# Attention weights of two batches turned by DMA in two float16 parts, batch 0 masked like the others, and the second w_out read once

## The chip, the cores and the metric

One core of one Trainium2 chip. The metric is the device time of one execution in microseconds (us); the time given for a kernel is the median of several runs.

## What is computed

Attention over 4 batches of 8 heads, 576 positions, 64 columns per head: heads 0 to 3 look at the last 32 positions (local), heads 4 to 7 at every 32nd (strided). Its output, 2304 tokens of 512 columns, goes through two layers of two products each, 512 to 2048 and back.

```python
scores = np.where(masks, scale * (q @ k.T), -1e9)      # per head
attn = np.exp(scores - scores.max(-1)); attn /= attn.sum(-1) + 1e-9
x = attn @ v                                           # (2304, 512)
h = x @ w_in;  x = np.maximum(0.01 * h, h) @ w_out     # first layer (moe)
h = x @ w_in2; x = (np.maximum(h, 0) + np.log1p(np.exp(-abs(h)))) @ w_out2
```

The weights arrive as 64-bit floats.

## The kernel before

The accuracy asked for is that of float32, so each large product is made of three float16 products, of a high and a low part of each side (`mm3`, lines 543 to 546). The weights are cut into such parts on the core: a quarter of a matrix (2 MB) is loaded, its largest value found (L169), its words shifted and merged (L175, L214 to L235), and the high and low parts written (L243, L250 to L258).

The attention of a batch goes in six halves: three local ones of four tiles of 96 rows by 128 columns for each of two partition groups, and three strided ones with tiles of 126, 108 and 108 rows (`spec`, L329). A half goes through these steps, each on its engine:

- `dots` (TensorE, L346): scores in float32, into a PSUM pair.
- `top` (VectorE, L381): the row maxima. In mode "e" a masked minimum (L395) also writes the masked, negated scores to a buffer `s` in SBUF, of which there are two. Batch 0 has the modes "pppaaa" instead: the mask is added on TensorE by a matmul (L362), VectorE takes one reduction for the whole half (L387), and in "p" TensorE lowers the scores by the maxima in PSUM (`lower`, L412).
- `expo` or `expos` (ScalarE, L437, L419): exponentials, per tile with the row sums in "e" and "a", in one instruction for the half in "p", where VectorE sums afterwards (L435).
- `guard`, `norm` (VectorE), `spread` (GpSimd, L466): division by the sums, L469.
- `turn` (TensorE, L471): float32 transposes of the weights into PSUM (L478), `fetch` (ScalarE, L481): a copy to SBUF (L489).
- `pv` (TensorE, L492): the output, L501; `high` and `rest` (L526, L533) cut it into float16 parts, the input of the first layer.

The first layer takes the 8 units of 288 tokens in turn: `plan_first` (L905) projects up (tile h), `plan_second` and `plan_second_by_f` project down (tile o). The second layer takes 9 units of 256 tokens (class `Unit`, L1190), with seven products in place of eight in its second matmul, for which sums of the quarters of w_out are cut into parts as well (L1095 to L1160). Its w_out is read twice: `plan_largest` (L877) loads all four quarters for one largest value, and the loop at L1147 loads each once more.

The order of the work is written out at build time: the class `Plan` (L585) simulates the engines with the costs that stand beside each step, and at each moment takes the ready step of the lowest rank (RANKS, L40: a start and a slope per kind of step). Each engine and SP's DMA queue then carries out its list in that order, and each step waits for what it reads. Where the plan finds TensorE idle in the first 130 us it puts in filler matmuls (`idle`, L97); ten more run at the start (WARM). The plan counts 2.6 us from the end of a load's queue time to its landing (LOAD, L588).

Of the kernel before, what the change touches and what calls it, by code (L numbers as in the profile page):

```python
# [9 lines left out]
BF16 = mybir.dt.bfloat16  # L10
# [22 lines left out]
SETS = [(0, 2), (2, 2), (4, 1)]  # L33
NEG = -8.0e9
TINY = 2.0 ** -100
WARM = 10
# [22 lines left out]
MODES = ("pppaaa","eeeeee","eeeeee","eeeeee")  # L59
# [4 lines left out]
def build(tc, qt, kl, ks, v, wi1, wo1, wi2, wo2, mloc, mstr, out):  # L64
    nc = tc.nc
    with ExitStack() as ctx:
# [37 lines left out]
        ml = const.tile([BLK, 4, WIN], BF16, name="ml")  # L104
        ms = const.tile([P, 234], BF16, name="ms")
        nc.scalar.dma_start(ml, mloc)
        nc.scalar.dma_start(ms, mstr)
# [160 lines left out]
        class Attn:  # L268
            def __init__(self, b):

                self.b, self.mode = b, MODES[b]
                self.q, self.k = {}, {}
                self.ps, self.sm, self.st, self.sv = {}, {}, {}, {}

            def load_qk(self, p, q=None, k=None):
                b = self.b
                w = S + STR if p < 2 else S
# [3 lines left out]
                nc.sync.dma_start(q[:, :S], qt[b, p])  # L281
# [47 lines left out]
            def spec(self, half):  # L329

# [1135 lines left out]
```

## Time and profile before

| | |
|---|---|
| median of 3 runs | 839.45 us (839.22 to 839.84) |
| the profiled execution | 838.91 us |
| its span, first to last instruction | 837.1 us |
| granted TensorE clock, mean | 0.998 of 2.4 GHz |
| TensorE matmuls busy | 825.3 us, 99% |
| VectorE busy | 486.1 us, 58% |
| ScalarE busy | 523.3 us, 63% |
| GpSimd busy | 256.0 us, 31% |

The profile names lines of the kernel before, engines and tiles. PE is TensorE, DVE VectorE, ACT ScalarE, POOL GpSimd, SP the queue that issues the loads and stores. The end of a matmul is modelled, so that neighbours overlap; the time that a group of matmuls takes on the engine is read from its start to the start of the next.

### The profile page before, as it was taken

The numbers are of one execution on the slowest core, as the hardware profiler recorded it, in microseconds if no ns is written. First come the engines' busy times: TensorE is split into PE (matmuls) and PEld (weight loads), VectorE is DVE, ScalarE is ACT, GpSimd is POOL, SyncE is SP. The second block draws the span as 40 slices with busy tenths as digits, with TensorE's granted clock in tenths as the row PEclk, the third lists the DMA queues.
The fourth block names the chain that finished last, engine by engine and source line by source line (L and its number), as shares of the span: only waits on it lengthen the run. The fifth ranks groups of instructions, "written<-read, shape, count | busy, mean of one in ns | idle before, by whom it ended". The sixth has DMA issues, their size and how long they took to land.

```text
span 837.1 us, 17534 instructions
## 1 busy us (share of the span) xinstructions
PE 825.3 (99%) x7323; PEld 681.8 (81%) x7323; DVE 486.1 (58%) x1134; ACT 523.3 (63%) x961; POOL 256.0 (31%) x193
## 2 busy tenths in 40 slices
PE   9999999999999999999999999999999999999997
PEld 4567777787788787777777888888888888888886
DVE  5999759630433262577535567867474755565453
ACT  2898958233765465135535398877667677787671
POOL 2248786112334432002414033222322232222220
PEclk9999999999999999999999999999999999999999
DMA  9934130300225520450202200000000000000000
GB/s 369 381 130 160 60 143 1 139 1 1 65 92 220 202 101 16 187 188 16 101 2 101 101 2 1 27 1 27 1 27 1 27 1 27 26 2 26 2 26 26
DMA packets 10991, 63.27 MB, mean 76 GB/s; under 512 B 1344, under 2 KB 1440, under 8 KB 7840
## 3 DMA queue, kind: packets, MB, share of 16 engines
q1 hardware_dynamic: 10656, 62.00, 19.6%
q8 instruction: 57, 0.93, 0.5%
q14 instruction: 22, 0.18, 0.1%
q10 hardware_dynamic: 256, 0.16, 0.1%
HBM read 57.44 MB, written 4.72 MB: 74 GB/s over the span
## 4 chain that ended last, share of the span: by engine, by line
PE 85%; ACT 5%; DMA 5%; DVE 4%; issue 0%; SPq 0%; POOL 0%; DVEq 0%; ACTq 0%
PE o L544 13%; PE o L546 13%; PE o L545 13%; PE h L544 13%; PE h L546 13%; PE h L545 13%; DMA v<-v_dram 3%; PE po L501 2%; PE ps L367 2%; PE pt L478 1%; DMA pair<-wi_dram 1%; ACT s L447 1%; ACT gr L1281 1%; DVE pair L224 1%; DVE pair L1317 1%; DVE pair L235 1%
## 5 line engine op out<-in xcount | busy, mean ns | idle before, releaser
L544 PE MATMUL h<-x,w 128*128 128x256 f16 (+1 forms) x1088 | 303.5, 279 | 0.9 <-ACT t L565 0.9
L546 PE MATMUL h<-x,w 128*128 128x256 f16 (+1 forms) x1088 | 303.4, 279 | 0.0
L545 PE MATMUL h<-x,w 128*128 128x256 f16 (+1 forms) x1088 | 303.4, 279 | 0.0
L1269 POOL TENSOR_TENSOR pair<-pair,t 128x512 f32<-128x512 f32 x72 | 93.9, 1304 | 270.7 <-ACT t L1265 123.2
L571 POOL TENSOR_TENSOR g<-t,g 128x576 f16<-128x576 f32 x64 | 99.9, 1567 | 202.4 <-ACT g L568 202.4
L546 PE MATMUL o<-g,pair 128*128 128x288 f16 x512 | 146.4, 286 | 0.8 <-DVE pair L258 0.8
L544 PE MATMUL o<-g,pair 128*128 128x288 f16 x512 | 146.5, 286 | 0.0
L545 PE MATMUL o<-g,pair 128*128 128x288 f16 x512 | 146.4, 286 | 0.0
L1285 DVE SCALAR_TENSOR_TENSOR gr<-pair,x2b,gr 128x896 f16<-128x896 f32 x72 | 87.2, 1212 | 83.5 <-ACT gr L1281 83.3
L545 PEld LDWEIGHTS <-w 128*128 128x128 f16 x1088 | 106.5, 98 | 19.7 <-issue 1.0
L544 PEld LDWEIGHTS <-w 128*128 128x128 f16 x1088 | 106.4, 98 | 19.6
L546 PEld LDWEIGHTS <-w 128*128 128x128 f16 x1088 | 106.4, 98 | 19.2
L1277 DVE TENSOR_TENSOR pair<-pair 128x128 f32<-128x128 f32 x288 | 71.7, 290 | 36.1 <-POOL pair L1269 33.6
L1281 ACT ACTIVATE gr<-pair,x2b 128x896 f16<-128x896 f32 x72 | 74.4, 1035 | 17.8 <-DVE pair L1277 15.2
L565 ACT ACTIVATE t<-h,gs 128x576 f32<-128x576 f32 x64 | 47.2, 737 | 60.6 <-PE h L546 55.5
L1252 ACT ACTIVATE t<-h,x2s 128x512 f32<-128x512 f32 x72 | 49.0, 680 | 52.0 <-PE h L546 52.0
L469 POOL TENSOR_TENSOR s<-s,sm 96x512 f32<-96x512 f32 (+3 forms) x48 | 47.8, 1016 | 89.9 <-DVE sm L464 40.6
L545 PE MATMUL o<-w,gr 128*128 128x256 f16 x270 | 73.6, 273 | 0.0
L544 PE MATMUL o<-w,gr 128*128 128x256 f16 x270 | 73.6, 273 | 0.0
L546 PE MATMUL o<-w,gr 128*128 128x256 f16 x270 | 73.6, 273 | 0.0
L169 DVE TENSOR_REDUCE m<-pair 128x1 f32<-128x2048 f32 x16 | 36.4, 2276 | 52.7 <-DMA pair<-wo_dram 37.6
L546 PEld LDWEIGHTS <-pair 128*128 128x128 f16 x512 | 50.1, 98 | 13.8 <-DVE pair L258 1.1
(134 smaller groups left out, 1367.7 us busy)
## 6 DMA issues: line engine op xcount, KB each, us to landing
pair<-wo_dram SPq DMA_DIRECT2D x12, 2048.0 KB, 8.1
pair<-wi_dram SPq DMA_DIRECT2D x8, 2048.0 KB, 10.9
out_dram<-pair SPq DMA_DIRECT2D x18, 256.0 KB, 2.1
q<-qt_dram SPq DMA_DIRECT2D x12, 288.0 KB, 4.0
v<-v_dram SPq DMA_DIRECT2D x2, 1408.0 KB, 14.9
pair<-v_dram SPq DMA_DIRECT2D x2, 1408.0 KB, 7.1
k<-ks_dram SPq DMA_DIRECT2D x7, 288.0 KB, 4.9
k<-kl_dram SPq DMA_DIRECT2D x5, 304.0 KB, 3.9
```

Of the source, the lines that this page charges most:

```text
L169: nc.vector.tensor_reduce(out=m, in_=hi.bitcast(F32), axis=AX.XY, op=ALU.max, apply_absolute_value=True)
L469: nc.gpsimd.tensor_tensor(out=sv, in0=sv, in1=rs, op=ALU.mult)
L544: nc.tensor.matmul(ps, ah, bh, start=first, stop=False)
L545: nc.tensor.matmul(ps, ah, bl, start=False, stop=False)
L546: nc.tensor.matmul(ps, al, bh, start=False, stop=last)
L565: nc.scalar.activation(t, ps, AF.Prelu, scale=gates[f // 4], alpha=0.01)
L571: nc.gpsimd.tensor_tensor(out=g[:, 1, f : f + 2, :], in0=t, in1=g[:, 0, f : f + 2, :], op=ALU.subtract)
L1252: nc.scalar.activation(t, self.ps[k], AF.Prelu, scale=self.sc[:, k // 2 : k // 2 + 1], alpha=-1.0)
L1269: nc.gpsimd.tensor_tensor(out=r, in0=r, in1=self.a[k], op=ALU.add)
L1277: nc.vector.tensor_tensor(out=r[:, o], in0=r[:, x], in1=r[:, y], op=op)
L1281: nc.scalar.activation(self.a[k][:, 0], self.r[k][:, 1:], AF.Copy, scale=self.ag)
L1285: nc.vector.scalar_tensor_tensor(out=a[:, 1], in0=self.r[k][:, 1:], scalar=self.ag, in1=a[:, 0], op0=ALU.mult, op1=ALU.subtract)
```

## The change

Six things.

1. Batches 2 and 3 (TURNED) have no `turn` and `fetch`. After `spread`, `cut` writes the weights of a half as float16 (ScalarE), `remain` the rest as a second float16 part over the bytes of the buffer `s` (VectorE), and `cross` turns each part by a transposing DMA on SP's queue, from SBUF to a region behind the batch's v. `join` adds the two turned parts back to float32 (VectorE), and `pv` reads that. One such region exists (place "tr"). The buffer `s` is held until `pv`; before it was held until the second `turn`. Strided tiles are read with 128 columns and 128 or 112 rows, and `guard`, `factor`, `high` and `rest` carry the scale in another place.
2. Batch 0 has mode "e" in all halves, so that the masks and the lowering on TensorE go.
3. The first loads of q and k are split: the columns of the first two local tiles first (`load_early`, k on ScalarE's queue), the rest later (`load_late`). WARM is 8, and the plan lets TensorE begin at 4.4 in place of 5.7.
4. `plan_largest` goes: each quarter of the second w_out is loaded once, with its own largest value, scale and broadcast matmul; the ratio of the scales is put on the activations (`self.ag` per quarter).
5. Some buffers move (q and k of batches 0 and 1, parts of the second w_out).
6. All ranks are new, and with them the order of the work.

Code for smaller tiles (SMALL, an empty tuple) is added and not used; it is left out below.

```diff
-WARM = 10
+WARM = 8
+TURNED = (2, 3)
+PAD = 20
 RANKS = {
-    "A2": (1411.761, 0.020), "B2": (870.957, 132.683), "B3": (-3104.685, 0.471), ...
+    "A2": (921.068, 0.024), "B2": (1213.392, 0.020), "B3": (-892.057, 7.138), ...
-MODES = ("pppaaa","eeeeee","eeeeee","eeeeee")
+MODES = ("eeeeee",)*4
...
+            def load_early(self):
+                for p, masks in ((0, [(mn, msml)]), (1, [(ml, mloc), (ms, mstr)])):
+                    self.q[p], self.k[p] = (get() for get in self.spots[p])
+                    n, m = 2 * BLK, 2 * BLK + STR
+                    nc.sync.dma_start(self.q[p][:, :n], qt[0, p][:, :n])
+                    nc.scalar.dma_start(self.k[p][:, :m], kl[0, p][:, :m])
+                    for mask in masks:
+                        nc.scalar.dma_start(*mask)
...
                 t0, nt = SETS[half - 3]
-                r = CLS[t0] * NJ
-                return r, r, [
+                r = w = CLS[t0] * NJ
+                if self.turned:
+                    r, w = -(-r // 16) * 16, P
+                return r, w, [
...
+            def cut(self, half):
+                r, w, tiles = self.spec(half)
+                n = len(tiles)
+                hi = att.tile([P, 512], F32, name="a", tag="aT", bufs=3)
+                self.hl[half] = both = [y.bitcast(F16)[:, : 2 * n * P] for y in (hi, flat(self.s[half]))]
+                self.cuts = [y[:r].rearrange("p (j n w) -> p j n w", j=2, n=n)[:, :, :, :w] for y in both]
+                nc.scalar.activation(self.cuts[0], self.sv[half], AF.Copy)
+
+            def remain(self, half):
+                hi, lo = self.cuts
+                nc.vector.tensor_tensor(out=lo, in0=self.sv[half], in1=hi, op=ALU.subtract)
+
+            def cross(self, half, i):
+                r, w, tiles = self.spec(half)
+                n, rows = len(tiles), -(-r // 16) * 16
+                y = self.hl[half][i]
+                t = self.hl[half][i] = self.across[:, i, : 2 * n * rows].rearrange("p (n r) -> p n r", r=rows)
+                nc.sync.dma_start_transpose(t, y[:rows])
+
+            def join(self, half):
+                r, w, tiles = self.spec(half)
+                n, (hi, lo) = len(tiles), self.hl[half]
+                a = flat(self.s[half])[:w, : 2 * n * r].rearrange("p (n r) -> p n r", r=r)
+                nc.vector.tensor_tensor(out=a, in0=hi[:w, :, :r], in1=lo[:w, :, :r], op=ALU.add)
+                for j in range(2):
+                    self.st[2 * half + j] = a[:, n * j : n * j + n]
...
-                clock = collections.defaultdict(float, SP=1.4, PE=5.7)
+                clock = collections.defaultdict(float, SP=1.4, PE=4.4)
...
+                if A.turned:
+                    y = [step("Pool", 0.05 + n / 4, A.spread, [norm], half, j) for j in range(2)]
+                    y = step("ACT", 0.12 + c / 1200, A.cut, y, half, take=["a"])
+                    y0 = step("SP", 0.8, A.cross, [y, ld["v"]], half, 0, take=["tr"], behind=chain["tr"])
+                    chain["tr"] = [y0]
+                    y1 = step("DVE", 0.1 + c / 960, A.remain, [y], half, port=True)
+                    y1 = step("SP", 0.8, A.cross, [y1], half, 1, behind=[y0])
+                    y1 = step("DVE", 0.1 + 2 * n * r / 960, A.join, [y0, y1], half, port=True, free=[y, y0])
+                    pv = step("PE", 0.1 + 0.19 * n, A.pv, [y1, ld["v"]], half, take=["po"], free=[held])
...
-        def plan_largest(W, name, busy):
...
-        o2_scaled = plan_largest(O2, "O2", busy)
...
+            ld = plan.add("SP", 5.15, lambda q=q: O2.load(q, area(1)), busy[1], ("LO2", q))
+            x = plan.add("DVE", 2.2, big, [ld], ("O2", q))
+            y = plan.add("PE", 0.06, over, [x], ("O2", q), take=["pt"])
+            sc = plan.add("DVE", 1.1, scale, [y], ("O2", q + 0.3), free=[y])
+            o2_scaled.append(sc)
             y = step("DVE", 1.14, lambda q=q: O2.low(q), [ld], 0.1)
-            y = sink(step, O2, q, lambda: late["o2s"], [y, o2_scaled], 0.3)
+            y = sink(step, O2, q, lambda st=st: st["s"], [sc, x, y], 0.3)
```

## Rows read from the trace of the kernel before

**Rows 1.** The page: engine, busy us, share of the span, instructions.

```profile
PE 825.3 (99%) x7323; PEld 681.8 (81%) x7323; DVE 486.1 (58%) x1134; ACT 523.3 (63%) x961; POOL 256.0 (31%) x193
```

**Rows 2.** Stages: window, length, busy us (instructions) per engine, clock, DMA share, GB/s.

```profile
0.00:61.00 61.00, 56.98 (x469) 33.72 (x470) 50.07 (x134) 39.84 (x124) 18.30 (x23) 1.00 0.76 300
61.00:92.00 31.00, 30.09 (x295) 23.99 (x296) 29.40 (x81) 27.05 (x77) 23.20 (x16) 1.00 0.30 111
...
180.00:255.00 75.00, 74.83 (x723) 60.26 (x721) 22.97 (x163) 45.18 (x162) 22.35 (x22) 1.00 0.19 64
...
300.00:335.00 35.00, 35.00 (x358) 27.89 (x356) 18.69 (x83) 20.78 (x63) 7.56 (x8) 1.00 0.05 12
335.00:540.00 205.00, 204.84 (x1739) 169.61 (x1737) 125.29 (x189) 112.26 (x137) 45.07 (x30) 1.00 0.19 74
```

**Rows 3.** Waits of TensorE, the longest: us in total, times, longest.

```profile
PE pt L478 <- ACT a L489: 1.7, 5, 0.6
```

**Rows 4.** Timeline of TensorE, first and last turn behind the front: start, length.

```profile
181.21 0.50 PE L478 MATMUL pt<-ident,s 96*128 96x96 f32 x4
181.63 1.12 PE L367 MATMUL ps<-k,q 64*96 64x128 f32 x16
...
330.19 0.35 PE L478 MATMUL pt<-ident,s 108*108 108x108 f32 x2
330.38 0.29 PE L544 MATMUL o<-g,pair 128*128 128x288 f16 x1
```

**Rows 5.** The first 61 us, three lines alone: filler L101, masks L362, lowering L412.

```profile
0.00:61.00 61.00, 22.82 (x84) 8.00 (x84) 1.00 0.76 300
...
0.00:61.00 61.00, 3.35 (x12) 1.29 (x12) 1.00 0.76 300
...
0.00:61.00 61.00, 5.57 (x12) 1.79 (x12) 1.00 0.76 300
```

**Rows 6.** Timeline of the front: first issue, filler, scores, reduction, first projection.

```profile
0.74 0.37 SPq L281 DMA_DIRECT2D v<-qt_dram  x1
...
1.62 5.14 PE L101 MATMUL idle<-idb 128*128 128x512 bf16 x15 [1.62 <-DVE idb L92]
...
7.13 1.12 PE L367 MATMUL ps<-v 64*96 64x128 f32 x16
...
8.29 1.22 DVE L387 TENSOR_REDUCE mx<-ps 96x8 f32<-96x1024 f32 x1 [6.73 <-PE ps L367]
...
54.84 0.30 PE L544 MATMUL h<-x,w 128*128 128x288 f16 x1
```

**Rows 7.** Groups by form: line, engine, shapes, count, busy us, mean ns.

```profile
L435 DVE TENSOR_REDUCE sm<-s 96x8 f32<-96x1024 f32 x3 | 3.6, 1209 | 0.0
L387 DVE TENSOR_REDUCE mx<-ps 96x8 f32<-96x1024 f32 x3 | 3.6, 1203 | 7.1 <-PE ps L367 7.1
...
L447 ACT ACTIVATE s<-s,mx 96x128 f32<-96x128 f32 x72 | 27.8, 389 | 0.0
...
L425 ACT ACTIVATE s<-ps 96x1024 f32<-96x1024 f32 x3 | 3.1, 1019 | 11.8 <-PE ps L412 11.8
L447 ACT ACTIVATE s<-ps,mx 126x126 f32<-126x126 f32 x8 | 2.8, 374 | 0.0
```

**Rows 8.** Timeline of VectorE: two masked minima in a row.

```profile
40.24 0.28 DVE L395 CUSTOM_DVE_ANT_0 s<-ps,ml 96x128 f32<-96x128 f32 x1
40.45 0.28 DVE L395 CUSTOM_DVE_ANT_0 s<-ps,ml 96x128 f32<-96x128 f32 x1
```

**Rows 9.** Landing of 288 KB loads (L281, 200 to 260 us), then of 256 KB stores (L1336).

```profile
DMA to landing us min/median/max: 2.8/3.3/5.0
...
DMA to landing us min/median/max: 2.0/2.1/3.1
```

**Rows 10.** The page's DMA issues: KB each, us from issue to landing.

```profile
v<-ks_dram SPq DMA_DIRECT2D x1, 288.0 KB, 7.8
```

**Rows 11.** Groups of GpSimd: the division by the sums.

```profile
L469 POOL TENSOR_TENSOR s<-s,sm 96x512 f32<-96x512 f32 (+3 forms) x48 | 47.8, 1016 | 89.9 <-DVE sm L464 40.6 <-DVE g L137 29.3 <-ACT s L447 11.7
```

More of the change, by code (lines that the diff above doesn't have):

```diff
@@ L366, in dots @@
                         js = slice(D * j, D * j + D)
+                        if self.small:
+                            for o in range(2):
+                                nc.tensor.matmul(
+                                    pv[js, o, i, :], self.q[p + o][js, q0 : q0 + QT], self.k[p + o][js, k0 : k0 + w],
+                                    start=not masked, stop=not masked or i == n - 1,
+                                )
+                            continue
                         nc.tensor.matmul(
@@ L475, in turn @@
                 pt = ps_pt.tile([P, 512], F32, name="pt", tag="pt")
+                self.st[2 * half + j] = pt
+                if self.small and half > 2:
+                    for i in range(n):
+                        o = i * w - (QT - w) * (i == n - 1)
+                        for h in range(2):
+                            hs = slice(QT * h, QT * h + QT)
+                            nc.tensor.matmul(
+                                pt[hs, QT * i : QT * i + QT], sv[hs].rearrange("p n w -> p (n w)")[:, o : o + QT], ident[hs, hs],
+                                start=True, stop=True,
+                            )
+                    return
                 ptv = pt[:w, : n * r].rearrange("p (n r) -> p n r", n=n)
@@ L717, in plan_loads @@
                 if n == "v":
-                    ld[n] = plan.add("SP", 3.4, lambda: A.load_v(buf()), after.get("v", ()), (f"L{b}", k))
+                    ld[n] = plan.add("SP", 4.6 if A.small else 3.4, lambda: A.load_v(buf()), after.get("v", ()), (f"L{b}", k))
+                    continue
+                if b == 0 and n < 2:
+                    A.spots = where
+                    cost, load = ((0.43, A.load_early), (2.3, A.load_late))[n]
+                    ld[n] = plan.add("SP", cost, load, after.get(n, ()), (f"L{b}", k), behind=[ld[0]] if n else [])
                     continue
@@ L875, in plan_quarter @@
             return step("DVE", 2.3, lambda: W.rest(q), [y], 0.6, port=True), sc
-        def plan_largest(W, name, busy):
-            m = once(lambda: sml.tile([P, 4], F32, name="m4", tag="wm4"))
-            st, read = {}, []
-            for q in range(4):
-                ld = plan.add("SP", 5.15, lambda q=q: W.load(q, area(1)), busy[1], ("L" + name, q))
-                y = plan.add("DVE", 2.2, lambda q=q: W.largest(q, m()[:, q : q + 1]), [ld], (name + "l", q))
-                busy[1] = [y]
-                read.append(y)
-            def over():
-                st["m"] = sml.tile([P, 1], F32, name="m", tag="wm")
-                nc.vector.tensor_reduce(out=st["m"], in_=m(), axis=AX.X, op=ALU.max)
-            def all_over():
-                st["g"] = to_all(st["m"])
-            def scale():
-                late["o2s"] = keep([P, 1], "s_o2")
-                nc.vector.tensor_copy(late["o2s"], W.scale_all(largest_of(st["g"])))
-            step = lambda eng, cost, fn, deps, **kw: plan.add(eng, cost, fn, deps, (name + "l", 4), **kw)
-            t = step("DVE", 0.1, over, read)
-            t = step("PE", 0.1, all_over, [t], take=["pt"])
-            return step("DVE", 1.1, scale, [t], free=[t])
         gs, xs = {}, {}
@@ L1181, in w2_join @@
         def w2_join():
+            c, m = late["co"], late["uo"] = keep([P, 4], "c_o2"), keep([P, 1], "u_o2")
+            for q in range(4):
+                nc.vector.tensor_copy(c[:, q : q + 1], O2.u[q])
+            r = sml.tile([P, 1], F32, name="r", tag="jr")
+            nc.vector.tensor_reduce(out=m, in_=c, axis=AX.X, op=ALU.max)
+            nc.vector.reciprocal(out=r, in_=m)
+            nc.vector.tensor_scalar(out=c, in0=c, scalar1=r, scalar2=None, op0=ALU.mult)
             late["u2"] = keep([P, 4], "u_w2")
```

296 lines of the change are left out of this document (206 added, 90 removed), and 20 rows, old and new, of the table RANKS.

## The prediction

> **What bounds the kernel now.** I read the page's busy shares first, then the busy time stage by stage, then the waits, then single stretches of the timeline. TensorE is busy for 825.3 of 837.1 us [rows 1]. That share alone does not show that its work is useful, so the stages come next [rows 2]: from 92 us to the end TensorE is full (74.83 of 75, 35.00 of 35, 204.84 of 205 in the three stretches shown), while VectorE and ScalarE have room in the stretches that hold the attention of batches 2 and 3 (VectorE 22.97 of 75 and 18.69 of 35 us). The waits agree: the largest that TensorE spends on another engine is 1.7 us in total, for the copy of turned weights [rows 3]. So behind the front every instruction taken from TensorE is worth its own slot, and every wait put in front of one costs its length.
>
> The front is different. Up to 61 us TensorE is "busy" with 84 filler matmuls (22.82 us), 12 mask matmuls (3.35) and 12 lowering matmuls (5.57) [rows 5]; the first projection starts at 54.84 [rows 6]. There VectorE is the full engine (50.07 of 61 us, idle until 8.29; then 29.40 of 31), with ScalarE close behind from 61 us on (27.05 of 31) [rows 2, 6]. TensorE work removed from the front is replaced by filler and gains nothing by itself; the front shortens only if the first projections come earlier.
>
> **The base.** The profiled execution took 838.91 us, 1.81 beside its span of 837.1; the median of the runs is 839.45, 0.54 above it. I change the trace by differences and take them off the median.
>
> **Part 1, turning by DMA in batches 2 and 3.** Removed from TensorE: 24 groups of transposes at L478. The first starts at 181.21 and the next instruction at 181.63, so it takes 0.42 us; the last takes 330.38 - 330.19 = 0.19 [rows 4]. Over all 24 groups these slots, from one start to the next, add up to 9.0 us; the busy times beside them (0.50 and 0.35) are longer because their modelled ends overlap the next instruction. All of it lies where TensorE is full: -9.0. Removed with them are 24 copies at L489, off the path.
>
> Added to TensorE: strided scores grow from 126 and 108 to 128 columns and strided outputs from 126 and 108 to 128 and 112. A group of 16 score matmuls at 128 columns takes at most 1.12 us [rows 4]. One set of a batch is short by 2 of 128 columns and two by 20 of 128, and the last is half as large: about 0.25 us per batch, 0.5 for both (0.3 to 0.8).
>
> Added elsewhere, twelve times: a cast of 1,024 columns on ScalarE (the nearest row, L425 of that size, 1.02 us), a subtraction and an addition on VectorE (a 1,024-column operation, L435, 1.21 us) [rows 7], and two transposing DMAs on SP's queue. The ScalarE casts (12) roughly repay the removed copies. VectorE gets 12 x 2.2 = 26 us in stretches where it stood idle for 68 of 110 us [rows 2]. Hidden.
>
> What is not hidden for certain is **latency**. The output matmuls of a half now wait for scores, VectorE, ScalarE, GpSimd (two at 1.02 us [rows 11]), cast, two DMAs and an addition, and they stand in an order written out by the planner. Whatever is behind them on TensorE, projections that are ready included, waits with them. The planner prices a transpose at 0.8 us of queue and 2.6 to land, 3.4 in all. No transposing DMA is in this trace. The nearest rows: 288 KB loads in this same stretch land 2.8 to 5.0 us after issue, median 3.3, and 256 KB stores 2.0 to 3.1, median 2.1 [rows 9]; the slowest of that size, stuck behind others at the start, took 7.8 [rows 10]. A transpose moves 192 KB within SBUF in a local half, 256, 224 and 112 in the three strided ones. Two score buffers keep two halves in flight, so lateness L - 3.4 shows at every second output group: 12 x (L - 3.4) / 2 = 6 x (L - 3.4). At 2.0 or 3.3 us this is 0, at 5.0 it is 9.6, at 7.8 it is 26.4. I take L = 3.7, since the loads of this stretch are the nearest row and a transpose is likely to be a little worse than a copy: +2 (0 to 26).
>
> SP's queue also holds these waits: the second transpose of a half waits for VectorE, and the loads of batch 3 and of the second layer's weights stand behind it. They have tens of us until use, so 0.
>
> **Part 2, batch 0 like the others, first loads split.** Masks and lowering leave TensorE in the front: 0 by themselves. On VectorE a local half cost two reductions, 1.20 + 1.21, and now costs eight masked minima at 0.21 (40.24 to 40.45) = 1.68: 0.7 less in each of three halves [rows 7, 8]. The strided halves I take as even (0.7 either way). ScalarE pays: a local half cost one exponential of 1.02 and now costs eight of 0.389, so 3 x 2.09 = 6.3 more, and the strided 20 some 0.3 more: +6.6 [rows 7]. It fits into the part of the front where ScalarE waits (39.84 of 61 us busy), unless it lands after 40 us. The start: filler runs from 1.62 for 5.14 us, the first scores start at 7.13 and VectorE's first reduction at 8.29 [rows 6]. Two fillers fewer and no mask matmul, with 96 KB pieces to wait for in place of four 288 to 304 KB loads, put this some 1.5 to 2.5 us earlier. The two k pieces and three masks, one of them unused, are now five issues of about 0.4 us on ScalarE's queue; its first exponential is later than 8.29, so they hide. VectorE is continuously loaded after it, so its gain is 2 + 2.2 = 4; I take -3.5 for the start of the projections, with -8 and +4 as ends. The better end is a front in which VectorE does batch 0 and the first quarter of the weights before anything of batch 1; the worse has ScalarE's 6.6 us on the path, less the start.
>
> **Part 3, w_out of the second layer read once.** Four loads of 2 MB go; the four reductions stay but move into each quarter, with three more scale steps and three more broadcast matmuls. These matmuls are smaller than a pair of turns, 0.19 [rows 4]: at most 0.6, taken as 0.3. TensorE loses 0.16 us in 335 to 540 [rows 2], so fewer loads can give no more than that; taken as 0. The cover is the first layer's last units. If it failed, TensorE would wait at the new broadcast matmul of a late quarter for VectorE, a few reductions of 2 us long.
>
> **Sum.** 839.45 - 9.0 + 0.5 + 0.3 - 3.5 = 827.75; with +2 of stalls, **829.8 us**.
>
> By a rule of the Trainium skill, "VectorE: DVE Perf Modes", section "The three transpose paths", one 128 x 128 bf16 transpose takes 390 ns on TensorE and 1,309 ns by DMA, and its "Rules for kernel authors" prefer TensorE where PSUM will do. The page's time for eight such blocks in a row would be an estimated 10.5 us, and the sum with it 827.75 + 6 x 7.1 = 870. No run here shows a transposing DMA yet.
>
> **Rivals.**
>
> *The transposes are late (slower).* If the queue handles the 128-column blocks of a transpose as DMAs of their own, eight issues of 0.37 us each [rows 6] take 3.0 before the last can land in 2.1 to 3.3: L = 5.1 to 6.3. The loss is 6 x 1.7 = 10 to 6 x 2.9 = 17, up to 26 at the slowest row: 838 to 854, 845 in the middle. It decides from L = 3.4 + 11.7 / 6 = 5.35 us. For it speaks that every output group has TensorE's whole queue behind it; against it that plain transfers of this size land in 2 to 5 us. Chance 0.25, of which 0.01 faster, 0.05 the same, 0.19 slower.
>
> *Blocks wholly one after the other (slower).* Each of eight waits for the one before to land, at least 8 x 2.0 = 16 us if like the shortest store: 6 x 12.6 = 76, some 900 us; at half that, about 855. The skill's section above bears on this one. Chance 0.04.
>
> *ScalarE takes over the front.* It is already full from 61 to 92 us [rows 2]. If the added 6.6 us fall there and only the early start of 2 is kept, the front is 4 longer: 827.75 + 3.5 + 4 = 835, with stalls 837. Still faster. Chance 0.12. This also stands for new ranks that order the front worse than the old ones.
>
> *A better front.* The end of -8 and no stalls: 823, down to 819. Chance 0.08.
>
> **How the numbers follow.** The forecast (824 to 835) has 0.51. About 0.2%, 1.7 us, is what a measurement of this kernel can tell from no change. Faster: 0.51 + 0.01 + 0.12 + 0.08 = 0.72; same 0.05; slower 0.19 + 0.04 = 0.23. The range goes from 819 to 848: it leaves out the upper part of the late transposes, the serial ones and a little of the better front, some 0.15.
>
> **What would show it.** Right: no transposes on TensorE behind the front; output matmuls of batches 2 and 3 with waits of some tenths of a us; transposing DMAs landing in 3 to 4 us; the first projection near 51 us; VectorE's first masked minimum near 6. Wrong in the large term: TensorE waits of a us or more for the addition after the second transpose, at up to twelve places, or filler-free idle slots between 180 and 335 us. Wrong in the front: a first projection later than 55 us, or TensorE gaps until 92 us that end with ScalarE. Wrong in part 3: TensorE waiting for a reduction of w_out between 335 and 540 us.

## The result, and the profile after

| | before | after |
|---|---|---|
| median | 839.59 us | 849.04 us (847.35 to 851.22) |
| ratio, 95% interval | | 1.0115 (1.0095 to 1.0136) |
| profiled execution, its span | 838.91, 837.1 us | 847.35, 845.3 us |
| TensorE matmuls busy | 825.3 us | 818.2 us |

(The 839.59 of before are from runs on the same chip.) The kernel is 1.15% slower. TensorE has 7.1 us less to do and takes 8.2 us longer. The page's line of busy times after the change, and the windows of [rows 2] again (window, length, busy us of PE, PEld, which is the weight load, DVE, ACT and POOL, then clock, DMA share, GB/s):

```profile
PE 818.2 (97%) x7228; PEld 672.8 (80%) x7228; DVE 519.6 (61%) x1280; ACT 531.1 (63%) x994; POOL 271.9 (32%) x193
```

```profile
0.00:61.00 61.00, 52.60 (x411) 32.03 (x412) 43.63 (x173) 41.25 (x138) 20.04 (x22) 0.94 0.80 313
61.00:92.00 31.00, 29.29 (x266) 22.25 (x265) 29.39 (x80) 28.01 (x65) 25.96 (x11) 1.00 0.34 121
180.00:255.00 75.00, 73.72 (x689) 57.59 (x688) 35.02 (x148) 38.34 (x121) 22.13 (x19) 1.00 0.27 62
300.00:335.00 35.00, 34.40 (x295) 27.02 (x291) 18.59 (x37) 20.05 (x34) 14.01 (x12) 1.00 0.43 140
335.00:540.00 205.00, 198.39 (x1674) 163.06 (x1673) 134.92 (x226) 106.25 (x130) 42.06 (x29) 1.00 0.14 52
```

Two windows stand out against [rows 2]: the first, where VectorE gets 6.4 us less done (43.63 for 50.07) and the clock is 0.94, and the last, where TensorE had 0.16 us of gaps and now has 6.6. The waits of TensorE over the whole run (us in total, times, longest), in place of the 1.7 of [rows 3]:

```profile
PE ps L409 <- DVE mx L447: 5.3, 3, 3.9
PE pm L142 <- DVE m L179: 4.8, 2, 3.1
PE po L611 <- DVE s L585: 2.9, 4, 1.0
```

L409 are the scores, L447 the masked minimum, L142 a broadcast matmul, L179 the largest value of a quarter, L611 the output, L585 the addition of the turned parts.

Where the time goes is read best from a count. Both kernels start the same projection matmuls (6,312 recorded in each, L544 to L546 before, L676 to L678 after). The start of the n-th after the change less that before is the lag at that point. At n = 600 the same share of the attention is done in both (192 of 352 score matmuls, 176 of 352 output matmuls), at n = 2000 all of it.

| n-th projection matmul | 0 | 200 | 600 | 1000 | 2000 | 2800 | 3000 | last |
|---|---|---|---|---|---|---|---|---|
| before, us | 54.8 | 92.9 | 142.0 | 193.5 | 345.3 | 443.4 | 467.9 | 831.1 |
| lag after | -3.6 | -5.6 | +5.1 | +3.9 | +1.0 | +3.7 | +8.7 | +8.2 |
| lag, mask first | -9.3 | -11.7 | -1.0 | -2.3 | -4.7 | -1.6 | +5.5 | +5.0 |
| lag, best version (below) | -9.2 | -11.6 | -0.8 | -2.1 | -5.4 | -5.3 | -3.2 | -2.9 |

Each row is one execution, and executions of one version lie 1 to 6 us apart (847.35 to 851.22 for the kernel after). So a lag is good to about 1 us at n = 600, and to less at the end: the two other versions below that keep the late mask and differ from the kernel after in later work only have +3.9 and +4.0 at n = 600, and all versions with the mask first have -1.4 to -0.3, apart from one (+1.2) that also changes other loads.

So the front lost 5.1 us, the attention of batches 2 and 3 gained 4.1 (from +5.1 to +1.0), and the second layer's w_out lost 7.2 (from +1.0 to +8.2): together the 8.2 by which the spans differ. The first projection at 51.26 us, earlier than 54.84 [rows 6], says nothing: the new order starts projections before the attention of batch 1, which then comes between them.

The second account is TensorE's time up to the 2000th projection matmul, each instruction from its start to the next start. Idle time of over 0.15 us before an instruction is counted as waiting:

| us of TensorE | before | after | mask first | best version |
|---|---|---|---|---|
| projections | 247.1 | 248.8 | 248.6 | 248.4 |
| scores | 22.9 | 25.4 | 24.7 | 24.9 |
| masks and lowering (L362, L412) | 8.2 | 0 | 0 | 0 |
| turns | 17.8 | 8.9 | 8.9 | 8.9 |
| outputs, broadcasts | 21.8 | 21.7 | 21.6 | 21.6 |
| filler | 21.6 | 27.0 | 25.0 | 24.8 |
| waiting | 4.2 | 12.9 | 10.2 | 9.6 |
| waiting behind the 2000th | 0.2 | 6.6 | 7.3 | 1.7 |

### The profile page after: what moved, and what is told of

It reads as the page before. It is cut to its first block, busy times and chain, and to the rows that moved or that the text cites. A ratio compares the mean times of both kernels' runs of the same rounds, so it can differ in the third digit from the quotient of the medians.

```text
span 845.3 us, 17556 instructions
## 1 busy us (share of the span) xinstructions
PE 818.2 (97%) x7228; PEld 672.8 (80%) x7228; DVE 519.6 (61%) x1280; ACT 531.1 (63%) x994; POOL 271.9 (32%) x193
## 4 chain that ended last, share of the span: by engine, by line
PE 75%; DVE 11%; DMA 6%; ACT 4%; issue 1%; POOL 1%; SPq 0%; DVEq 0%; POOLq 0%; ACTq 0%
PE o L676 12%; PE o L678 12%; PE o L677 12%; PE h L676 11%; PE h L678 11%; PE h L677 11%; DMA pair<-wo_dram 3%; PE ps L409 2%; PE po L611 2%; DMA pair<-s 2%; ACT s L499 2%; PE idle L109 1%; DVE m L179 1%; DVE pair L1249 1%; DVE pair L245 1%
## 5 line engine op out<-in xcount | busy, mean ns | idle before, releaser
L676 PE MATMUL h<-x,w 128*128 128x256 f16 (+1 forms) x1088 | 303.6, 279 | 1.1 <-ACT t L697 1.1
L677 PE MATMUL h<-x,w 128*128 128x256 f16 (+1 forms) x1088 | 303.4, 279 | 1.2 <-DVE x L672 1.2
L678 PE MATMUL h<-x,w 128*128 128x256 f16 (+1 forms) x1088 | 303.4, 279 | 0.0
L1421 POOL TENSOR_TENSOR pair<-pair,t 128x512 f32<-128x512 f32 x72 | 97.2, 1350 | 270.3 <-ACT t L1417 128.1
L676 PE MATMUL o<-g,pair 128*128 128x288 f16 x512 | 146.5, 286 | 0.8 <-ACT x L1080 0.8
L678 PE MATMUL o<-g,pair 128*128 128x288 f16 x512 | 146.4, 286 | 0.0
L677 PE MATMUL o<-g,pair 128*128 128x288 f16 x512 | 146.4, 286 | 0.0
L1437 DVE SCALAR_TENSOR_TENSOR gr<-pair,x2g,gr 128x896 f16<-128x896 f32 x72 | 86.7, 1206 | 79.0 <-ACT gr L1433 79.0
L676 PEld LDWEIGHTS <-w 128*128 128x128 f16 x1088 | 106.4, 98 | 21.1 <-issue 0.2
L678 PEld LDWEIGHTS <-w 128*128 128x128 f16 x1088 | 106.4, 98 | 20.8 <-issue 1.4
L677 PEld LDWEIGHTS <-w 128*128 128x128 f16 x1088 | 106.5, 98 | 20.0 <-issue 1.7
L525 POOL TENSOR_TENSOR s<-s,sm 96x512 f32<-96x512 f32 (+6 forms) x48 | 61.6, 1303 | 92.3 <-DVE sm L520 61.5
L1433 ACT ACTIVATE gr<-pair,x2g 128x896 f16<-128x896 f32 x72 | 74.4, 1035 | 11.4 <-DVE pair L1429 10.9
L499 ACT ACTIVATE s<-s,mx 96x128 f32<-96x128 f32 (+4 forms) x176 | 67.5, 387 | 11.6 <-DVE mx L447 11.6
L697 ACT ACTIVATE t<-h,gs 128x576 f32<-128x576 f32 x64 | 47.0, 734 | 43.9 <-PE h L678 42.4
L676 PEld LDWEIGHTS <-pair 128*128 128x128 f16 x512 | 50.1, 98 | 13.5 <-issue 0.2
L677 PEld LDWEIGHTS <-pair 128*128 128x128 f16 x512 | 50.1, 98 | 13.1 <-issue 0.9
L678 PEld LDWEIGHTS <-pair 128*128 128x128 f16 x512 | 50.1, 98 | 12.6
L678 PE MATMUL o<-pair,gr 128*128 128x256 f16 x198 | 54.0, 273 | 0.0
```

The costliest lines, as they stand in the source:

```text
L499: nc.scalar.activation(sv[:, i, :], src[:, i, :], AF.Exp, bias=mx[:, j, i : i + 1], scale=scale, accum_out=self.sm[half][:, j, i : i + 1],)
L525: nc.gpsimd.tensor_tensor(out=sv, in0=sv, in1=rs, op=ALU.mult)
L676: nc.tensor.matmul(ps, ah, bh, start=first, stop=False)
L677: nc.tensor.matmul(ps, ah, bl, start=False, stop=False)
L678: nc.tensor.matmul(ps, al, bh, start=False, stop=last)
L697: nc.scalar.activation(t, ps, AF.Prelu, scale=gates[f // 4], alpha=0.01)
```

## The experiments

In kernels with one line more, L410, L448, L586, L612, L677 and L698 are L409, L447, L585, L611, L676 and L697 of the kernel after. L676 is also the first of the three matmul lines of the projections; L697 is ScalarE's leaky ReLU of the first layer (it reads tile h), L1409 its ReLU in the second layer.

### The front: the local mask first on ScalarE's queue

The timeline of the kernel after, some rows of the first 14 us (start, length, engine, line, operation; ACTq is ScalarE's queue, in brackets the idle time before and what ended it), and the issue of the mask in the same stretch (KB, us to landing):

```profile
0.76 0.40 ACTq L302 DMA_DIRECT2D qk<-kl_dram  x1
1.19 0.45 ACTq L304 DMA_DIRECT2D qk<-msml_dram  x1
1.67 0.45 ACTq L302 DMA_DIRECT2D qk<-kl_dram  x1
3.75 0.34 ACTq L304 DMA_DIRECT2D ml<-mloc_dram  x1
...
8.18 1.12 PE L409 MATMUL ps<-qk 64*96 64x128 f32 x16
...
11.38 0.29 DVE L447 CUSTOM_DVE_ANT_0 s<-ps,ml 96x128 f32<-96x128 f32 x1 [9.81 <-DMA ml<-mloc_dram]
...
13.21 1.17 PE L409 MATMUL ps<-qk 64*96 64x128 f32 x8 [3.91 <-DVE mx L447]
```

```profile
ml<-mloc_dram ACTq DMA_DIRECT2D x1, 48.0 KB, 7.5
```

The first scores start at 5.15 us, but VectorE waits until 11.38 for 48 KB of mask, issued at 3.75 behind two pieces of k and a mask that nothing reads, and landing 7.5 us later among the large loads. TensorE runs out of score buffers and waits 3.91 us. The edit (mask first, the unused one not loaded):

```diff
-                for p, masks in ((0, [(mn, msml)]), (1, [(ml, mloc), (ms, mstr)])):
+                nc.scalar.dma_start(ml, mloc)
+                for p, masks in ((0, []), (1, [(ms, mstr)])):
```

> The changed kernel (849.0), with one thing moved: the local mask is the first load on ScalarE's queue, ahead of the two k pieces, and the unused third mask is not loaded. In the changed kernel's trace VectorE stood idle for 9.81 us on that mask and took its first masked minimum at 11.38 us; TensorE then waited 3.9 us and its granted clock fell to 0.56 between 15 and 20 us. Theory A, the late mask is what the front lost: the first minimum moves to 6 to 7 us, TensorE keeps its clock, and the time falls by 3 to 5 us, to about 845. Theory B, the new order of batch 1's attention is what the front lost, and the late mask is made good later: the minimum moves, but the time falls by less than 1.5 us.

Measured: 843.63 us (842.31 to 845.86) beside 839.47 before, ratio 1.0043 (1.0029 to 1.0057); 5.4 us back. Its mask and its first masked minimum:

```profile
ml<-mloc_dram ACTq DMA_DIRECT2D x1, 48.0 KB, 2.4
```

```profile
6.93 0.29 DVE L448 CUSTOM_DVE_ANT_0 s<-ps,ml 96x128 f32<-96x128 f32 x1 [5.36 <-PE ps L410]
```

VectorE now waits for the scores and starts 4.45 us earlier; the lag at the 600th matmul goes from +5.1 to -1.0, filler from 27.0 to 25.0 us and waiting up to there from 9.5 to 6.2. The first theory holds, with a little more than it said. The late mask was the whole loss of the front; that the unused mask is no longer loaded came with the same edit and was not tried by itself.

### Turning: undone in two versions

```diff
-TURNED = (2, 3)
+TURNED = ()
```

> The changed kernel without part 1: batches 2 and 3 are turned on TensorE again, with float32 transposes, and the rest is as changed (the order is planned anew from the same ranks). Theory A, turning by DMA is a gain of about the size that was forecast (9.0 off TensorE, 0.5 for wider tiles, 2 to 3 of waits): this kernel is 4 to 8 us slower than the changed one, 853 to 857. Theory B, late transposes and the waits behind them are why the change is slower: this kernel is 3 us or more faster than the changed one.

> The version with the early broadcast and the longer planned load, with no batch turned by DMA: all four batches turn on TensorE again. Theory A (the turning is worth what its undoing showed before, 3.3 us): 842 to 843.5. Theory B (the predicted 6.5, hidden there by other losses): 845 to 846.5. Theory C (nothing is left of it once the broadcast is mended): 838.5 to 840.

In the kernel after, undoing it gave 852.29 us (851.95 to 852.82): 3.3 slower. In the version with mask and broadcast mended (839.13, below) it gave 843.72 (842.11 to 844.73): 4.6 slower. Both are nearest to their first theory. So turning by DMA is a gain of 3.3 to 4.6 us, in both versions less than the predicted 6.5. Undoing it also writes a new order for all that follows. The stretch from the 600th to the 2000th matmul, which holds the attention of batches 2 and 3, shows the part by itself, and both pairs agree on 3.9 us there:

| us of TensorE, n = 600 to 2000 | kernel after | turning undone | mended version | turning undone |
|---|---|---|---|---|
| turns | 0 | 9.0 | 0 | 9.0 |
| waiting | 3.4 | 0.4 | 3.1 | 0.4 |
| projections | 174.1 | 172.9 | 174.2 | 172.9 |
| scores | 11.2 | 10.4 | 11.4 | 10.4 |
| outputs, broadcasts | 10.4 | 10.3 | 10.4 | 10.3 |
| together | 199.1 | 203.0 | 199.1 | 203.0 |

Of the waiting, 2.9 us in the kernel after and 2.4 in the mended version are for the addition of the turned parts:

```profile
PE po L612 <- DVE s L586: 2.4, 3, 1.0
```

The transposes landed as the plan had priced them (kernel after; KB are not given for these; median us to landing):

```profile
pair<-a SPq DMA_TRANSPOSE x12, 3.4
pair<-s SPq DMA_TRANSPOSE x12, 3.2
```

### The second w_out, read once

In the kernel after, the waits of TensorE between 335 and 540 us, one broadcast with what stands before and behind it, and VectorE at that time:

```profile
PE pm L142 <- DVE m L179: 4.8, 2, 3.1
PE h L676 <- ACT t L697: 1.1, 2, 0.6
PE o L676 <- ACT x L1080: 0.8, 1, 0.8
```

```profile
407.73 0.29 PE L678 MATMUL h<-x,w 128*128 128x288 f16 x1
409.74 0.23 PE L142 MATMUL pm<-idb,m 128*128 128x128 bf16 x1 [1.72 <-DVE m L179]
409.81 0.29 PE L676 MATMUL o<-g,pair 128*128 128x288 f16 x1
...
407.39 2.29 DVE L179 TENSOR_REDUCE m<-pair 128x1 f32<-128x2048 f32 x1 [7.78 <-DMA pair<-wo_dram]
```

VectorE waits 7.78 us for the quarter, reduces it for 2.29, and a broadcast matmul of 0.07 us holds up projections that are ready. A first edit planned the load longer (5.15 to 8.65 us), alone and with the mask first:

```diff
-            ld = plan.add("SP", 5.15, lambda q=q: O2.load(q, area(1)), busy[1], ("LO2", q))
+            ld = plan.add("SP", 8.65, lambda q=q: O2.load(q, area(1)), busy[1], ("LO2", q))
```

> The changed kernel with the planned queue time of each second w_out load raised from 5.15 to 8.65 us; nothing else in the work differs, only the place of the steps that follow these loads, the four new broadcast matmuls above all. The trace of the changed kernel has 6.6 us of TensorE idle time between 395 and 473 us, 4.8 of it at two broadcast matmuls that wait for VectorE's reduction of a loaded quarter. Theory A, the broadcast matmuls stand too early in TensorE's order: these waits go and the time falls by 4 to 6.5 us. Theory B, the quarters themselves are late, one after another: the wait moves to the cut parts of the last quarter, which the second layer's first unit needs, and the time stays within 1.5 us.

> The mask first and the later place of the second w_out's steps together. If both losses are what they seem and independent, the falls add up: 7 to 11 us below the changed kernel, 838 to 842. If only the broadcast matmuls matter, 843 to 845; if neither, 848 to 850.

Measured: 855.19 us (854.63 to 856.27) alone, 849.15 (847.83 to 850.96) with the mask first, 5.5 to 6.2 us slower than without the edit. The first theory's waits at the broadcasts go, but the time rises where it said it would fall. A new wait stands between 520 and 560 us (the version with the late mask):

```profile
PE h L676 <- ACT pair L1409: 8.7, 4, 3.3
```

```profile
526.64 1.89 ACT L1267 ACTIVATE w<-pair 128x2048 f16<-128x2048 f32 x1
528.45 0.67 ACT L1409 ACTIVATE pair<-h,x2s 128x512 f32<-128x512 f32 x1
...
529.17 0.27 PE L676 MATMUL h<-x,w 128*128 128x256 f16 x1 [2.02 <-ACT pair L1409]
```

TensorE waits for ScalarE's ReLU of the second layer (L1409), which stands in ScalarE's list behind a cut of the last quarter's sums (L1267). These cuts end at 536.3 us here and at 516.9 in the kernel after. (The expectations call L1409 the cut sums.) The quarters share one area, so they follow one another; my reading is that the time granted to each load pushes the last quarter's steps back to where the second layer needs ScalarE. Next, part 3 was undone in the mask-first version (`plan_largest` back, one broadcast for all quarters, the loads as before the change). The new ranks have none for the step of that largest value, so one was set by hand (600):

> The mask-first version with part 3 undone: the second w_out is read twice again, one largest value, one broadcast matmul. Theory A (the lag of 7 to 10 us behind the 2800th float16 matmul is the four broadcasts, each behind a load and a reduction of its own): the waits for L179 at the broadcast go, the lag against the kernel before stays near the -4.7 that the mask-first run had at the 2000th projection matmul, 839.5 - 4.7 = 834.8, 833 to 837. Theory B (any version with these ranks loses there, because the quarters' own chain is late): the loss moves to another wait of the same stretch, 840 to 848. Theory C (the loads read twice now come late themselves): TensorE waits for w_out words behind the 3000th matmul, over 843.

Measured: 846.00 us (842.90 to 848.41), 2.4 above the version that reads once, with runs that overlap. The lag is 0.0 at the 2000th matmul in place of -4.7. Of this, 2.2 us are lost by the 600th (+1.2 for -1.0); the rest lies where the four extra loads stand between the transposes on SP's queue. Issues from 240 to 340 us, this version first, then mask first alone:

```profile
pair<-wo_dram SPq DMA_DIRECT2D x4, 2048.0 KB, 8.5
...
pair<-a SPq DMA_TRANSPOSE x7, 4.3
pair<-s SPq DMA_TRANSPOSE x7, 4.8
```

```profile
pair<-a SPq DMA_TRANSPOSE x7, 3.5
pair<-s SPq DMA_TRANSPOSE x7, 3.0
```

With the loads, transposes land 0.8 and 1.8 us later, and TensorE waits 5.4 us for the addition, once 2.4. The lag then grows by 7.1 us behind the 2000th matmul although only one broadcast is left there; TensorE waits for ScalarE and GpSimd instead (2.8, 1.5). So under these ranks a version that reads twice loses as much in that stretch, at other waits, as the second theory said. What share of it comes from the rank set by hand was not tried.

The place of the broadcast was tried next: ranked before all projections, with the old planned load (first) and with the longer one, 8.65 and 7.0.

```diff
-            y = plan.add("PE", 0.06, over, [x], ("O2", q), take=["pt"])
+            y = plan.add("PE", 0.06, over, [x], ("A3", 0), take=["pt"])
```

> The mask-first version with the broadcast matmuls of the second w_out ranked before all projections; the load's planned cost stays 5.15. Theory A (the place of the broadcast in TensorE's list is the fault; the first one moves 13 us forward and the chain with it): waits at L142 under 1 us and 838 to 840, as with place and cost both changed. Theory B (the load's planned cost is the fault: the list has the matmul before its load can have landed and been reduced, now even more so): the waits at the broadcast stay at 4 to 7 us in total, 842 to 845, and it took both edits together.

> The mask-first version, w_out read once, but the plan ranks the broadcast matmul of a quarter before all projections and counts 3.5 us more for its load. Theory A (it is only a matter of where the broadcast stands in TensorE's list): no wait at the broadcast above 1 us and no late quarter, 834 to 837, equal to the version that reads twice. Theory B (the chain of load, reduction, broadcast, scale, parts, sums is at its limit whenever each quarter must first be reduced): the waits at the broadcast go, but TensorE waits for the cut sums (L1409) between 500 and 560 us as it did with the margin alone, 843 to 852.

> The version with the early broadcast, planned cost of a quarter's load 7.0 in place of 8.65 (5.15 gave 842.97, 8.65 gave 839.13). Theory A (the margin matters smoothly): between the two, 839 to 843. Theory B (every changed cost writes another order, and the time moves by some us without a direction): outside that, 835 to 838 or 844 to 850.

Measured: 842.97 us (840.94 to 845.39) with 5.15, 839.13 (837.89 to 841.84) with 8.65, 837.16 (835.91 to 838.76) with 7.0; the last has the ratio 0.9971 (0.9961 to 0.9982). Place alone is worth 0.7; place and price together 4.5 to 6.5. The waits at L142 for L179 are 2.8 us with 5.15 and 0.2 and 0.5 with the others. Place alone goes as the second theory said (842 to 845, with waits of 2.8 us where it said 4 to 7); place with 8.65 lies between its two theories, without the wait at L1409; and that 7.0 is better than both 5.15 and 8.65 is what the theory of orders without a direction said (835 to 838). The version with 8.65 has a wait of its own at 440 us:

```profile
PE h L677 <- ACT t L698: 2.2, 1, 2.2
```

There ScalarE's list has the cut of the third quarter first, which waits for the sums on VectorE (L1250, 5.6 us, planned 2.5). Planning the sums at 5.6 in the version with 8.65:

```diff
-            sums = step("DVE", 2.5, lambda q=q: o2_sums(q), [y], 0.5)
+            sums = step("DVE", 5.6, lambda q=q: o2_sums(q), [y], 0.5)
```

> The version with the early broadcast and the longer planned load, and the planned cost of a quarter's sums on VectorE raised from 2.5 to 5.6 us, since the four L1250 operations took 2.6, 4.5, 5.6 and 2.6 there. Theory A (the 2.2 us that TensorE waits at 440 us for ScalarE's L698 come from ScalarE's list, in which the cut of the third quarter stands in front and waits for these sums): the wait goes, 836.5 to 837.5. Theory B (the chain has no slack; a later place for the cut makes its readers wait): the wait goes but the first projection that reads the cut sums waits 2 us or more, 839 to 843.

Measured: 850.01 us (847.69 to 853.26), 10.9 slower. Neither number held. The wait at 440 is gone, and two of twice its length stand in the new order (L1434 cuts the activations of the second layer on ScalarE; the trace is of the slowest run, 853.26):

```profile
PE pm L142 <- ACT t L698: 4.4, 1, 4.4
PE o L677 <- ACT gr L1434: 4.2, 1, 4.2
```

A price that fits the longest of the four sums, and is 3 us too long for two of them, gave a worse order: the planned cost acts here less as a size than as a choice of order.

### The transposes' price, and a version that beats both

The issue of a transposing DMA took 1.2 us on SP's queue, planned at 0.8:

```diff
-                    y0 = step("SP", 0.8, A.cross, [y, ld["v"]], half, 0, take=["tr"], behind=chain["tr"])
+                    y0 = step("SP", 1.25, A.cross, [y, ld["v"]], half, 0, take=["tr"], behind=chain["tr"])
-                    y1 = step("SP", 0.8, A.cross, [y1], half, 1, behind=[y0])
+                    y1 = step("SP", 1.25, A.cross, [y1], half, 1, behind=[y0])
```

> The version with the early broadcast and the longer planned load, and a transposing DMA planned at 1.25 us of queue in place of 0.8, since its issue took 1.2 us on SP's queue. Theory A (the 2 to 3 us that TensorE waits for the addition L586 and the 2.5 for the strided k come from transposes planned too short): these waits fall to under 1.5 together, 836 to 838. Theory B (a changed cost writes another order): 840 to 850.

> Both planned costs together: a quarter's load at 7.0 us and a transposing DMA at 1.25 us of queue, in the version with the mask first and the early broadcast. With the transposes priced at 1.25 the 2000th projection matmul came 1.0 us earlier than with 0.8; with the load at 7.0 the rest of the way lost 3.1 us against the kernel before, with 8.65 3.7 to 3.8. Theory A (the two gains lie in different stretches and add): 836 to 836.5. Theory B (a changed cost writes another order for all that follows): anything from 835 to 845, with a wait that neither had.

With the load at 8.65: 838.59 us (837.02 to 841.37). The wait for the addition falls from 2.4 to 0.9 us and the lag at the 2000th matmul from -5.0 to -5.9, as the first theory says, but the medians differ by only 0.5 us, within their spread, and L698 has 4.0 us of waits in place of 2.2. With the load at 7.0: **836.80 us** (835.39 to 837.69), ratio 0.9967 (0.9955 to 0.9980). This is the best version, 2.7 us faster than the kernel before; beside 837.16 the step itself is too small to be told, and it lies 0.3 outside what the theory of two gains that add allowed. Its windows from 180 us on, to be held against those above:

```profile
180.00:255.00 75.00, 74.88 (x704) 58.38 (x703) 38.52 (x166) 41.20 (x136) 24.24 (x20) 1.00 0.32 77
300.00:335.00 35.00, 35.00 (x291) 27.78 (x290) 21.11 (x33) 16.93 (x21) 9.72 (x7) 1.00 0.51 184
335.00:540.00 205.00, 203.18 (x1723) 167.90 (x1722) 129.78 (x232) 111.64 (x139) 44.12 (x31) 1.00 0.12 45
```

### One part alone in the kernel before

Four versions of the kernel before: modes of batch 0 alone, turning alone, w_out read once alone, and the new ranks alone.

> The kernel before with batch 0 in mode e alone; loads, ranks and all else as before. Theory A (the front is bound by VectorE and ScalarE as counted in the prediction, and masks on TensorE are replaced by filler): VectorE 2.2 us less, ScalarE 6.6 us more, in old ranks: 836 to 842, within 3 us of the kernel before. Theory B (batch 0 in mode e costs the front its lead, because the first eight exponentials per half wait for one another on ScalarE): 842 to 848.

> The kernel before with the turning by DMA in batches 2 and 3 alone, old ranks, old loads, w_out read twice. Theory A (the gain is what the undo of the turning showed, 3.3 to 4.4 us): 835 to 836. Theory B (the predicted -6.5, with the rest lost only to the other parts): 832 to 834. Theory C (the turning needs its own ranks): TensorE waits for the addition L585 with the old ranks, 838 or more.

> The kernel before with part 3 alone: each quarter of the second w_out loaded once, with its own largest value, broadcast matmul and scale; old order, old places of the parts, all else as before. Theory A (reading once costs by itself, since every quarter's reduction and broadcast come between its load and its parts): TensorE waits at the broadcasts or for the cut sums between 335 and 540 us, 843 to 850. Theory B (the loss of that stretch belongs to the new order; the prediction's +0.3 was right for the part itself): 838 to 840.5.

> The kernel before with the new ranks alone (w_out read twice, batch 0 in its old modes, turning on TensorE). Theory A (the new order costs by itself what is lost after the 2000th projection matmul, 4 to 7 us): 843 to 848, with TensorE waits between 335 and 540 us where the kernel before has 0.2. Theory B (an order fits only the work it was made for; under old work the new ranks disturb the front as well): over 850. Theory C (the new ranks are as good as the old): 838 to 841.

Measured: 852.41 us (851.10 to 853.60), 886.48 (885.07 to 888.61), 923.39 (922.56 to 924.59) and 874.28 (871.17 to 875.28). Modes alone is slower than either theory said. Of turning alone only the third theory is left (TensorE waits for the addition, 18.0 us in all), of the new ranks alone the second (over 850; the lag is already +18.1 at the 600th matmul); reading once alone has the waits of its first theory, at the broadcasts, and a far larger loss. Turning alone: the old ranks leave the last halves of batch 3 until nothing else is ready, so that TensorE waits out their chain (window 372 to 406, and two of its waits; L542 is the output and L529 the addition there):

```profile
372.00:406.00 34.00, 10.35 (x102) 8.14 (x101) 16.45 (x71) 13.81 (x50) 5.21 (x6) 0.60 0.19 37
```

```profile
391.22 1.97 PE L542 MATMUL po<-s,pair 128*64 128x128 f32 x16 [10.05 <-DVE s L529]
...
404.95 1.01 PE L542 MATMUL po<-s,pair 128*64 128x112 f32 x8 [5.90 <-DVE s L529]
```

Read once alone: the first quarter is loaded at 371.5 us, as in the kernel before (370.7), but the fourth 178 us later, there 99, and three broadcasts wait for a whole quarter each (L132 is the broadcast, L169 the reduction):

```profile
PE pm L132 <- DVE m L169: 75.7, 3, 26.3
```

Two of these waits are 26.3 us long, 26.6 from one broadcast to the next, with no other matmul between them: that is the length of one quarter's chain from area to area, four times 26.6 = 106 us that must start early enough. In the kernel after the four loads start 45.9, 27.9 and 30.7 us apart. Modes alone: filler up to the 2000th matmul is 35.6 us in place of 21.6, and waiting 7.4 in place of 4.2. New ranks alone: 13.0 us more of waiting up to there, 7.6 of it in one wait for a turned copy. These four measure an order that was made for other work, not the part.

## Why the prediction was wrong

Forecast 829.8 us (819 to 848) and faster; measured 849.04 and slower. By its steps:

*The turns (right).* -9.0 was predicted; 17.8 - 8.9 = 8.9 us of TensorE left. The wider tiles were right too: from one start to the next a set of 108 rows takes 0.95 us before and 1.06 to 1.07 with 128 columns (mask first), the half set 0.56 and 0.62 to 0.63, some 0.4 for both batches.

*The stalls of part 1 (mechanism right, size off).* L was 3.2 to 3.4 us, better than the 3.7 assumed, so the formula 6 x (L - 3.4) gave 0. Yet where the part stands it is worth 3.9 us and not 6.5 (the table above). TensorE waits 2.7 to 3.0 us more where 2 was forecast. Scores and outputs take 0.9 to 1.1 more where 0.5 was. And 1.2 to 1.3 us, for which the sum had no term, lie in the projections: 9 score groups follow a projection there, none in the versions with the turning undone, where a turn or an output stands in front of them. The projection in front of scores takes 0.23 us from start to start, one in front of another projection 0.12, so 1.0 us in all. Single landings ran from 2.4 to 6.0 us, and a wait falls where one is late, not by the median. SP's queue, costed at 0, has a share: the strided k of batch 3, issued between transposes, made TensorE wait 0.6 us in the kernel after, 1.4 to 1.8 in three other orders. (The 7.8 us of [rows 10] was not the slowest load of its size: a 288 KB load issued at 11.2 us landed after 23.4. No transpose came near either.) The rivals of late and of serial transposes fall. By the Trainium skill, "VectorE: DVE Perf Modes", section "The three transpose paths", eight blocks would have been an estimated 10.5 us; the trace has 3.2 to 3.4 for up to eight 128 x 128 blocks in one transfer, so that rate does not add up block by block here.

*The front (wrong sign).* The failed sentence is that the five issues on ScalarE's queue "hide" behind its first exponential. It counted 0.4 us of issue each and left out who waits for the landing: VectorE's first minimum needs the mask, which landed at 11.25. -3.5 became +5.1. With the mask first the front gave -1.0 (the 600th matmul). The 8.2 us of masks and lowering are gone, and up to the 600th matmul 3.4 of them came back as filler, 3.0 as waiting and 1.1 as longer scores, as the prediction said of TensorE work in the front. VectorE stays the full engine there. It starts at 6.93 for 8.29 and has 77.9 us of work up to 92 us for 79.5: 3.0 of the 4 us that were counted. Only 1.0 of the 3.5 taken reached the projections. One lead is that VectorE's masked minima wait 2.0 us there for a turn to free a buffer `s`, which they don't in the kernel before; it was not tried. "ScalarE takes over the front" did not happen, though ScalarE's work up to 92 us grew by 7.5 us (74.4 for 66.9, mask first; 6.6 forecast): no wait of TensorE above 1.5 us in total names it before 335 us. And the marker, the start of the first projection, was badly chosen: it came out as predicted (51.26 for 51) while the front was late.

*w_out read once (+0.3 became +7.2).* The cover named, the first layer's last units, was no cover, because the broadcast stands inside TensorE's list among them: 4.8 of the 6.6 us of waits in that stretch are at two broadcasts. A load that lands after 7.7 us, a reduction of 2.3 and a chain of 26.6 us per quarter were not added up; from [rows 2] only the busy time was read, not the chain. What would show it wrong was named, and is what the trace shows. Mended, the stretch still loses 2.5 us in the best version (from -5.4 to -2.9).

*The new ranks (left out).* They were costed at nothing but a mention under a rival. Every version of the experiments that changed a planned cost moved the time by 0.4 to 11 us (the two smallest, 0.4 and 0.5, are within the noise), and each part under the ranks of the other kernel costs 13 to 84. How much of the +7.2 is order and how much the chain can't be told from these runs: reading twice under the new ranks, with one rank set by hand, loses as much (7.1), reading once under the old ones far more.

Of the 19.2 us between forecast and result, the mends gave back 12.2: 5.4 for the mask, 6.5 for the broadcast, 0.4 for the transposes' price, which the noise could hide. Of the 7.0 left to 829.8, by the lags of the best version, about 2.7 lie in the front (-0.8 for -3.5), 2 in the attention of batches 2 and 3 (-4.6 for -6.5) and 2.2 in w_out (+2.5 for +0.3).

## What to carry to other kernels

For each load that a change moves, ask for its landing and for its first reader, not for its issue time; 48 KB of mask behind three other pieces cost 5.4 us. A tiny matmul that needs a reduction is as long as everything in front of that reduction, for all that stands behind it in an in-order list. Where a planner writes the order, a part can't be priced by taking it alone out of the trace: compare lags at equal work done, and leave room for the order itself.

## What the runs showed of the hardware

A transposing DMA within SBUF of 112 to 256 KB, issued on SP's queue, took 1.2 us to issue (1.19 to 2.74) and 3.2 to 3.4 us to land in the median (2.4 to 6.0), 4.3 to 4.8 in the median where four 2 MB loads shared the stretch.

After the wait of 3.91 us in the front of the kernel after, with TensorE busy 1.79 of 5 us, the granted clock fell towards the lower of its two levels (1.2 of 2.4 GHz) for some us, although TensorE was full again (windows as above):

```profile
10.00:15.00 5.00, 1.79 (x16) 1.68 (x16) 3.53 (x33) 3.29 (x17) 0.00 (x0) 0.75 1.08 417
15.00:20.00 5.00, 5.00 (x17) 1.84 (x14) 3.53 (x5) 2.98 (x16) 3.29 (x4) 0.56 1.01 432
```

With the mask first it stays at 1.00 over the first 61 us. In the version that reads once alone, with TensorE busy 0.58 of 27 us, it was at the lower level all through:

```profile
506.00:533.00 27.00, 0.58 (x2) 0.21 (x2) 14.95 (x21) 5.37 (x4) 0.00 (x0) 0.50 0.21 78
```

A matmul that waits holds up ready ones behind it: the broadcast at 409.74 us of the kernel after came after 1.72 us of idle time, and the projection behind it started 0.07 us later. The Trainium skill, "PSUM — Partial Sum Buffer", section "Engine vs sequencer instructions", says that matmuls start and complete in program order; the trace agrees.

VectorE's 128 x 512 subtractions of the sums took 678 to 1,762 ns each, the same instruction in the same kernel (early broadcast, load at 8.65). The five of 1,647 to 1,762 ns ran while GpSimd was at its subtraction L704, the eleven of 678 to 693 with GpSimd idle. The third and the fourth quarter's four:

```profile
431.52 3.68 POOL L704 TENSOR_TENSOR g<-t,g 128x576 f16<-128x576 f32 x2 [24.85 <-ACT g L701]
432.40 5.62 DVE L1250 TENSOR_TENSOR pair<-pair 128x512 f32<-128x512 f32 x4
435.58 1.29 POOL L704 TENSOR_TENSOR g<-t,g 128x576 f16<-128x576 f32 x1 [0.39 <-ACT g L701]
...
471.22 2.62 DVE L1250 TENSOR_TENSOR pair<-pair 128x512 f32<-128x512 f32 x4
```

No run moved GpSimd's step away from them, so that it is the cause is read from this overlap alone.
